# The K-times-probability products of a decode step: one broadcast VectorE instruction of 2048 columns in place of eight of 256

## The chip, the cores and the metric

The kernel runs on one core of one Trainium2 chip. The metric is the device time of one execution in microseconds (us); lower is better. A run's number is the median of its repeated executions.

## The reference

One token passes through attention with a key and value cache, then a gated feed-forward block, and the gradients of everything are wanted as well. The cut that matters:

```
G = 8 groups of 2 query heads, Dh = 256, Sk = 32768 cache rows, only the last W = 4096 rows take part
p  = softmax(q k^T / 16)            # per head, over the 4096 rows
o  = p v ;  out = ... wo ... feed-forward ...
outputs: out_0 (the token), out_1 (its gradient), out_2 and out_3 (gradients of the K and V cache,
         each 8 x 32768 x 256 in bf16, zero outside the last 4096 rows), out_4 .. out_8 (of the weights)
```

So most of the output is zeros: 235 of the 281 MB that the kernel writes are the 28,672 untouched rows of each head group in out_2 and out_3.

## The kernel before

It has three parts. Zero fills of out_2 and out_3 run from the first microseconds to nearly the end; GpSimd issues them. Meanwhile part one goes through the eight groups of heads: scores of a group, softmax, then its "moments" (M = V^T diag(p) K per head, from which later gradients come cheaply). Part two is the projection and the feed-forward. Part three makes the cache gradients of the 4096 rows and the weight gradients and stores them.

The part that the change touches:

```python
        def moments(g, p_f):
            K_sb, V_sb = kv_at(K_off[g]), kv_at(V_off[g])
            M_ps = ps_m.tile([128, 2, 2 * Dh], f32, tag="M")
            for c in range(8):
                pK = pK_slot[c % 2]                    # two buffers of 2048 bf16 columns
                for i in range(4):
                    t = 4 * c + i
                    for hh in range(2):
                        nc.vector.tensor_scalar(out=pK[:, i, hh, :], in0=K_sb[:, t, :], scalar1=p_f[:, 8 * i + c, hh:hh + 1], scalar2=None, op0=ALU.mult)
                for i in range(4):
                    t = 4 * c + i
                    for vh in range(2):
                        nc.tensor.matmul(M_ps[:, vh, :], lhsT=V_sb[:, t, vh * 128:(vh + 1) * 128], rhs=pK[:, i, :, :]..., ...)
            for k, X_sb in enumerate((V_sb, K_sb)):
                for t in range(T):
                    nc.tensor.matmul(ok_ps[:, k, :], lhsT=ppad[g % 2][...], rhs=X_sb[:, t, :], ...)
            # [...] M_ps is copied out
        # [...]
        p_next = scores(0)
        for g in range(G):
            p_f = p_next
            if g + 1 < G:
                p_next = scores(g + 1)
            moments(g, p_f)
            # [...] loads of later K and V; of wo after the last groups
```

The zero fills:

```python
HALF0, HALF1 = 42, 55
    # [...]
    send_fills(0, HALF0)              # each 2 MB, from the whole zeros tile
    send_fills(HALF0, HALF1, True)    # each 2 MB, from the first half of the zeros tile, read twice
    # [...] the second half of the tile meanwhile holds feed-forward weights
            if n == 1:                                          # second block of the feed-forward done
                nc.vector.memset(ar(ZW // 2, ZW // 2), 0.0)     # the second half becomes zeros again
                send_fills(HALF1, len(fills))
```

And the last stage ends with five more zero transfers on SyncE's queue, 18 MB in sum. The order of the instructions on each engine is set by a scheduler when the kernel is built, not by the text above alone.

Of the kernel before, what the change touches and what calls it, by code (L numbers as in the profile page):

```python
# [10 lines left out]
ALU = mybir.AluOpType  # L11
# [6 lines left out]
Dh = 256  # L18
# [15 lines left out]
def kernel(  # L34
        ctx, tc, A_x, A_k_cache, A_v_cache, A_wq, A_wo, B_x, B_w_gate, B_w_up, B_w_down, grad_out,
           out_0, out_1, out_2, out_3, out_4, out_5, out_6, out_7, out_8):
    nc = tc.nc
# [18 lines left out]
    def kv_at(off):  # L56
        return ar(off, T * Dh).rearrange("p (t d) -> p t d", d=Dh)
# [181 lines left out]
    def fill_vpad(i, src):  # L239

        nc.vector.tensor_copy(out=vpad[i][:].rearrange("p e (c w) -> p e c w", w=18)[:, :, :, 0:2],
                              in_=src.unsqueeze(2).to_broadcast([128, 2, 8, 2]))

    def dots(X_sb, XT_slots, pad, rows, cols_pool, cols_tag, evac):

        rows_ps = ps_s.tile([16, 512], f32, tag="rows")
        for q in range(8):
            XT = XT_slots[q % 3]
            tr_ps = ps_tr.tile([128, 2, 4, 128], bf16, tag="tr")
            for dh in range(2):  # L250
                for i in range(4):
                    nc.tensor.transpose(tr_ps[:, dh, i, :], X_sb[:, 4 * q + i, dh * 128:(dh + 1) * 128], ident_bf[:])  # L252
            evac(q, XT, tr_ps[:])
            for dh in range(2):
                nc.tensor.matmul(rows_ps[:], lhsT=pad[:, dh, 16 * q:16 * q + 16], rhs=XT[:, dh].rearrange("p t k -> p (t k)"),  # L255
                                 start=(q == 0 and dh == 0), stop=(q == 7 and dh == 1))
        nc.vector.tensor_copy(out=rows, in_=rows_ps[:])
        cols_ps = cols_pool.tile([128, 4, 8, 2], f32, tag=cols_tag, name="cols_ps")
        for i in range(4):
            nc.tensor.transpose(cols_ps[:, i].rearrange("p c h -> p (c h)"), rows[:, i * 128:(i + 1) * 128], ident_f[0:16, 0:16])  # L260
        return cols_ps
    with tc.tile_pool(name="ps_m", bufs=1, space=bass.MemoryType.PSUM) as ps_m, \
            tc.tile_pool(name="ps_x", bufs=1, space=bass.MemoryType.PSUM) as ps_x, \
            tc.tile_pool(name="ps_c", bufs=1, space=bass.MemoryType.PSUM) as ps_c, \
            tc.tile_pool(name="work1", bufs=2) as work1:

        def scores(g):
            fill_vpad(g % 2, qT_bf[:, 4 * g:4 * g + 4].rearrange("p (k e) -> p e k", e=2))
            sT_ps = dots(kv_at(K_off[g]), KT_slot, vpad[g % 2], rows1, ps_c, "cols", lambda q, XT, ps: nc.scalar.copy(out=XT, in_=ps))  # L269
            pmax = small.tile([16, 1], f32, tag="pmax")  # L270
            nc.vector.reduce_max(out=pmax[:], in_=rows1, axis=AX)
            pmaxT_ps = ps_t.tile([1, 16], f32, tag="tmp")
            nc.tensor.transpose(pmaxT_ps[:], pmax[:], ident_f[0:16, 0:16])
            gmax = small.tile([1, 2], f32, tag="gmax")
            nc.vector.reduce_max(out=gmax[:], in_=pmaxT_ps[:].rearrange("o (c h) -> o h c", h=2), axis=AX)
            nc.vector.tensor_scalar(out=gmax[:], in0=gmax[:], scalar1=-SCALE, scalar2=None, op0=ALU.mult)
            nb_ps = ps_t.tile([128, 2], f32, tag="tmp")
            nc.tensor.matmul(nb_ps[:], lhsT=ones_f[0:1, 0:128], rhs=gmax[:], start=True, stop=True)
            nbias = small.tile([128, 2], f32, tag="nbias")
            nc.vector.tensor_copy(out=nbias[:], in_=nb_ps[:])  # L280
            e_f = work1.tile([128, T, 2], f32, tag="e_f")
            psums = small.tile([128, 2], f32, tag="psums")
            for hh in range(2):
                nc.scalar.activation(out=e_f[:, :, hh], in_=sT_ps[:].rearrange("p i c h -> p (i c) h")[:, :, hh], func=ACT.Exp, bias=nbias[:, hh:hh + 1], scale=SCALE,
                                     accum_out=psums[:, hh:hh + 1])
            tot_ps = ps_t.tile([128, 2], f32, tag="tmp")
            nc.tensor.matmul(tot_ps[:], lhsT=ones_f[:, :], rhs=psums[:], start=True, stop=True)
            rsum = small.tile([128, 2], f32, tag="rsum")
            nc.vector.reciprocal(out=rsum[:], in_=tot_ps[:])
            nc.vector.tensor_tensor(out=pT_all[:, g], in0=e_f[:], in1=rsum[:].unsqueeze(1).to_broadcast([128, T, 2]), op=ALU.mult)  # L290
            p_f = work1.tile([128, T, 2], f32, tag="p_f")
            nc.vector.tensor_copy(out=p_f[:], in_=pT_all[:, g])
            pp = ppad[g % 2]
            if g > 1:
                nc.vector.memset(pp[:, :, 2 * g - 4:2 * g - 2], 0.0)
            nc.vector.tensor_copy(out=pp[:, :, 2 * g:2 * g + 2], in_=pT_all[:, g])  # L296
            return p_f

        def moments(g, p_f):
            K_sb, V_sb = kv_at(K_off[g]), kv_at(V_off[g])  # L300
            M_ps = ps_m.tile([128, 2, 2 * Dh], f32, tag="M")
            for c in range(8):
                pK = pK_slot[c % 2]
                for i in range(4):
                    t = 4 * c + i
                    for hh in range(2):
                        nc.vector.tensor_scalar(out=pK[:, i, hh, :], in0=K_sb[:, t, :], scalar1=p_f[:, 8 * i + c, hh:hh + 1], scalar2=None, op0=ALU.mult)  # L307
                for i in range(4):
                    t = 4 * c + i
                    for vh in range(2):  # L310
                        nc.tensor.matmul(M_ps[:, vh, :], lhsT=V_sb[:, t, vh * 128:(vh + 1) * 128], rhs=pK[:, i, :, :].rearrange("p h d -> p (h d)"),  # L311
                                         start=(t == 0), stop=(t == T - 1))
            for k, X_sb in enumerate((V_sb, K_sb)):
                for t in range(T):
                    nc.tensor.matmul(ok_ps[:, k, :], lhsT=ppad[g % 2][:, 8 * (t % 4) + t // 4, :], rhs=X_sb[:, t, :],  # L315
                                     start=(g == 0 and k == 0 and t == 0), stop=(g == G - 1 and k == 1 and t == T - 1))
            for vh in range(2):
                nc.scalar.copy(out=M_sb[g][:, vh].rearrange("p h d -> p (h d)"), in_=M_ps[:, vh, :])  # L318

        def load_wo(n):  # L320
            LD.dma_start(out=wo_sb[:, 16 * n:16 * n + 16, :], in_=A_wo.rearrange("(p j) n -> p j n", j=32)[:, 16 * n:16 * n + 16, :])

        ok_ps = ps_x.tile([H, 2, Dh], f32, tag="ok")
        after = {0: [("K", 3), ("V", 3)], 1: [("K", 4), ("V", 4), ("K", 5)], 2: [("V", 5)], 3: [("V", 6), ("K", 6)], 4: [("K", 7)], 5: [("V", 7)]}
# [6 lines that stand above are left out]
            for kind, n in after.get(g, []):  # L331
                if kind == "K":
                    load_kv(K_off[n], A_k_cache, n)
                else:
                    load_kv(V_off[n], A_v_cache, n)
            if g == G - 2:
                load_wo(0)
        nc.vector.tensor_copy(out=ok_rows, in_=ok_ps[:])
# [19 lines left out]
    with tc.tile_pool(name="ps_mid", bufs=3, space=bass.MemoryType.PSUM) as ps_mid, \  # L358
# [34 lines left out]
        for n in range(len(BLOCKS)):  # L393
# [3 lines left out]
            for b in range(nb):  # L397
                nc.vector.tensor_tensor_reduce(out=dgb[:, 0:D], in0=wd[:, b, :], in1=dh2_bc[:], scale=1.0, scalar=0.0,
                                               op0=ALU.mult, op1=ALU.add, accum_out=d_hh[:, b0 + b:b0 + b + 1])
# [11 lines left out]
            for i in range(2):  # L411
                nc.vector.tensor_tensor(out=diag[:, 0:w].rearrange("p (m b) -> p m b", b=nb), in0=ident_f[:].unsqueeze(2).to_broadcast([128, 128, nb]),
                                        in1=dgu_f[:, i, cs].unsqueeze(1).to_broadcast([128, 128, nb]), op=ALU.mult)
# [6 lines left out]
            for c in range(4):  # L420
# [3 lines left out]
                                               op0=ALU.mult, op1=ALU.add, accum_out=dhn[0:kp, c, n:n + 1])  # L424
# [28 lines left out]
        for jc in range(32):  # L453
            nc.vector.tensor_tensor_reduce(out=wo_sb[:, jc, :], in0=wo_sb[:, jc, :], in1=dh_bc[:], scale=1.0, scalar=0.0,  # L454
                                           op0=ALU.mult, op1=ALU.add, accum_out=doX_f[:, jc:jc + 1])
# [3 lines left out]
                                in1=m8_f[:].unsqueeze(2).to_broadcast([128, 8, 32]), op=ALU.mult)  # L459
# [13 lines left out]
        for dh in range(2):  # L473
# [11 lines left out]
                                scalar1=SCALE, scalar2=None, op0=ALU.mult)  # L485
# [4 lines left out]
    with tc.tile_pool(name="work2", bufs=2) as work2, tc.tile_pool(name="lnw", bufs=1) as lnw, \  # L490
# [17 lines left out]
        for c in range(3):  # L508
            nc.vector.tensor_tensor_reduce(out=wq2A[:, c, :], in0=wq2A[:, c, :], in1=dq_bc, scale=1.0, scalar=0.0,  # L509
                                           op0=ALU.mult, op1=ALU.add, accum_out=dn1[:, c:c + 1])  # L510
        for h in range(2):
            nc.vector.tensor_tensor_reduce(out=wq2A[:, 0, 0:HJ], in0=wq2B, in1=dq_bc[:, h * HJ:(h + 1) * HJ], scale=1.0, scalar=0.0,
                                           op0=ALU.mult, op1=ALU.add, accum_out=dn1[:, 3 + h:4 + h])
# [86 lines left out]
        for it, g in enumerate(order):  # L600
# [3 lines left out]
            def evac(q, XT, ps):  # L604
                if q % 2:
                    nc.scalar.copy(out=XT, in_=ps)  # L606
                else:
# [7 lines left out]
                                    in1=delta_bc[:, 2 * g:2 * g + 2].unsqueeze(1).to_broadcast([128, T, 2]), op=ALU.subtract)  # L615
# [17 lines left out]
            for l in range(8):  # L633
                for qp in range(2):
# [5 lines left out]
                    t = 4 * l + 2 * qp  # L640
# [47 lines left out]
```

## Time and profile before

802.11 us, median of 3 runs (801.46 to 802.81).

| what | before |
|---|---|
| bytes moved, mean rate | 334.84 MB, 418 GB/s |
| TensorE, VectorE, ScalarE busy | 57%, 46%, 25% of the span |
| last VectorE instruction ends | 719.8 us of 800.5 |
| product stage | 59 to 301 us |

The transfers bound this kernel: no slice but the first and the last is under 409 GB/s. VectorE (DVE) waits 67 us in the product stage for TensorE to free a product buffer.

From the windows table of before, one whole group of heads, then the end of the run (stretch, its length, busy us of PE, PEld, DVE, ACT, POOL with counts, then the clock granted to TensorE, the DMA share, GB/s):

```profile
187.50:219.00 31.50, 31.31 (x224) 16.86 (x222) 15.39 (x75) 9.60 (x15) 3.20 (x6) 1.00 1.00 426
...
750.00:785.00 35.00, 0.00 (x0) 0.00 (x0) 0.00 (x0) 0.00 (x0) 0.00 (x0) 0.50 1.00 430
785.00:790.00 5.00, 0.00 (x0) 0.00 (x0) 0.00 (x0) 0.00 (x0) 0.00 (x0) 0.50 0.74 315
790.00:795.00 5.00, 0.00 (x0) 0.00 (x0) 0.00 (x0) 0.00 (x0) 0.00 (x0) 0.50 0.18 75
795.00:800.50 5.50, 0.00 (x0) 0.00 (x0) 0.00 (x0) 0.00 (x0) 0.00 (x0) 0.50 0.04 18
```

In the product stage TensorE is full and VectorE half full.

From the timeline of before (start us, length us, engine, line, what, count): 26 products in a row, the first five zero fills after GpSimd (POOL) had waited 26.28 us for the refill of the zeros tile, and the last VectorE instruction.

```profile
204.58 5.18 DVE L307 TENSOR_SCALAR arena<-arena,p_f 128x256 bf16<-128x256 bf16 x26
...
374.61 2.65 POOL L132 DMA_DIRECT2D out_dram<-arena  x5 [26.28 <-DVE arena L428]
...
719.12 0.68 DVE L646 CAST arena<-d_ps 128x512 bf16<-128x512 f32 x1
```

### The profile page before, as it was taken

How to read it: one execution, taken by the hardware profiler on the slowest of the kernel's cores; microseconds unless marked ns; L12 is line 12 of the kernel's file. 1: busy time of each engine (PE TensorE's matmuls, PEld its weight loads, DVE VectorE, ACT ScalarE, POOL GpSimd, SP SyncE). 2: the span in 40 equal slices, each digit the busy share in tenths (PEclk: the TensorE clock that was granted, in tenths of full speed). 3: DMA queues.
4: the chain of work that ended last, by engine and by line, in shares of the span. 5: the costliest groups of instructions: out<-in, count | busy, mean ns of one | idle time of the engine just before them, and what ended most of it. 6: DMA issues, size and time to landing. Idle time of an engine off the chain costs nothing.

```text
span 800.5 us, 8486 instructions
## 1 busy us (share of the span) xinstructions
PE 459.3 (57%) x3182; PEld 245.9 (31%) x3182; DVE 370.2 (46%) x1176; ACT 196.3 (25%) x309; POOL 62.0 (8%) x112
## 2 busy tenths in 40 slices
PE   0459999999999994623239295845262064520000
PEld 0334554545545552312129143322021022200000
DVE  2115363472552652255770975766681187660000
ACT  0143313224133100000002054643241045340000
POOL 4000000010100110101100010000000000000000
PEclk9978999999999997555559699776557567655555
DMA  9999999999999999999999999999999999999994
GB/s 350 431 430 429 428 430 430 427 428 428 431 426 422 428 417 409 420 422 428 433 423 425 424 430 428 429 426 426 424 427 423 426 420 425 423 424 427 423 440 192
DMA packets 29359, 334.84 MB, mean 418 GB/s; under 512 B 2819, under 2 KB 5894, under 8 KB 7814
## 3 DMA queue, kind: packets, MB, share of 16 engines
q0 software_dynamic: 16496, 216.01, 63.8%
q1 hardware_dynamic: 11382, 116.68, 34.7%
q10 hardware_dynamic: 1440, 1.61, 0.6%
q8 instruction: 25, 0.41, 0.2%
q14 instruction: 16, 0.13, 0.0%
HBM read 53.69 MB, written 280.59 MB: 418 GB/s over the span
## 4 chain that ended last, share of the span: by engine, by line
PE 35%; DMA 33%; DVE 15%; ACT 4%; issue 2%; another core or an unknown queue 0%; SPq 0%; ACTq 0%; DVEq 0%
DMA out_dram<-arena 19%; PE M_ps L311 11%; PE ok_ps L315 6%; PE rows_ps L255 6%; PE tr_ps L252 4%; DMA dh_bc<-in_grad_out_dram 4%; DMA arena<-in_A_k_cache_dram 4%; ACT arena L269 2%; DMA arena<-in_A_wo_dram 2%; DVE arena L645 2%; DVE arena L454 2%; DVE arena L646 2%; DMA arena<-in_B_w_up_dram 2%; PE dqb_ps L497 2%; DMA arena<-in_B_w_gate_dram 2%; DVE arena L509 2%
## 5 line engine op out<-in xcount | busy, mean ns | idle before, releaser
L307 DVE TENSOR_SCALAR arena<-arena,p_f 128x256 bf16<-128x256 bf16 x512 | 109.8, 280 | 67.0 <-PE M_ps L311 67.0
L311 PE MATMUL M_ps<-arena 128*128 128x512 bf16 x512 | 122.9, 381 | 0.0
L255 PE MATMUL rows_ps<-arena,vpad 128*16 128x512 bf16 x256 | 85.9, 431 | 22.2 <-DVE arena L608 16.9
L252 PE MATMUL tr_ps<-ident_bf,arena 128*128 128x128 bf16 x1024 | 87.9, 236 | 15.0 <-DMA arena<-in_A_k_cache_dram 8.4
L132 POOL DMA_DIRECT2D out_dram<-arena x90 | 48.8, 544 | 560.7 <-DMA out_dram<-arena 522.7
L252 PEld LDWEIGHTS <-arena 128*128 128x128 bf16 x1024 | 65.9, 105 | 65.0 <-issue 55.4
L638 PE MATMUL d_ps<-arena,rT 32*128 32x512 bf16 x256 | 43.6, 511 | 69.6 <-DVE arena L646 50.2
L269 ACT COPY arena<-tr_ps 128x1024 bf16<-128x1024 bf16 x64 | 61.7, 1015 | 87.9 <-PE tr_ps L252 87.9
L311 PEld LDWEIGHTS <-arena 128*128 128x128 bf16 x512 | 46.2, 99 | 50.8 <-issue 6.5
L315 PE MATMUL ok_ps<-arena 128*16 128x256 bf16 x512 | 57.5, 273 | 0.9 <-DVE arena L296 0.9
L606 ACT COPY arena<-tr_ps 128x1024 bf16<-128x1024 bf16 x32 | 32.5, 1016 | 96.1 <-PE tr_ps L252 39.3
L642 ACT CAST arena<-d_ps 128x512 bf16<-128x512 f32 x64 | 37.6, 588 | 71.5 <-PE d_ps L638 71.5
L645 DVE CAST arena<-d_ps 128x512 bf16<-128x512 f32 x64 | 43.9, 686 | 14.9 <-PE d_ps L638 14.6
L315 PEld LDWEIGHTS <-arena 128*16 128x16 bf16 x512 | 45.4, 90 | 13.9 <-issue 3.4
L646 DVE CAST arena<-d_ps 128x512 bf16<-128x512 f32 x64 | 43.5, 680 | 8.3 <-DMA out_dram<-arena 8.3
L638 PEld LDWEIGHTS <-rT 32*128 32x128 bf16 x256 | 11.2, 95 | 95.4 <-issue 52.1
L643 ACT CAST arena<-d_ps 128x512 bf16<-128x512 f32 x64 | 38.0, 594 | 9.1 <-DMA out_dram<-arena 9.1
L255 PEld LDWEIGHTS <-vpad 128*16 128x16 bf16 x256 | 18.9, 91 | 57.1 <-issue 49.3
L318 ACT COPY arena<-M_ps 128x512 f32<-128x512 f32 x16 | 8.6, 589 | 75.0 <-PE M_ps L311 75.0
L509 DVE CUSTOM_DVE_ANT_0 arena<-arena 128x4096 bf16<-128x4096 bf16 x3 | 13.1, 4422 | 23.1 <-ACT arena L502 23.1
L608 DVE COPY arena<-tr_ps 128x1024 bf16<-128x1024 bf16 x32 | 21.7, 680 | 4.1 <-PE tr_ps L252 4.0
L631 DVE TENSOR_SCALAR arena<-R_sb,tl_f 128x512 bf16<-128x512 bf16 x64 | 17.8, 347 | 2.1 <-ACT R_sb L628 1.9
(198 smaller groups left out, 358.1 us busy)
## 6 DMA issues: line engine op xcount, KB each, us to landing
out_dram<-arena POOLq DMA_DIRECT2D x103, 2048.0 KB, 53.5
out_dram<-arena SPq DMA_DIRECT2D x18, 2048.0 KB, 32.7
arena<-in_A_v_cache_dram SPq DMA_DIRECT2D x10, 2048.0 KB, 49.6
arena<-in_A_k_cache_dram SPq DMA_DIRECT2D x8, 2048.0 KB, 29.7
out_dram<-arena SPq DMA_DIRECT2D x4, 4096.0 KB, 57.2
arena<-in_A_wq_dram SPq DMA_DIRECT2D x2, 3072.0 KB, 20.5
arena<-in_A_wo_dram SPq DMA_DIRECT2D x2, 1792.0 KB, 16.2
out_dram<-arena SPq DMA_DIRECT2D x2, 1792.0 KB, 33.2
```

The lines of the kernel that those rows point to most:

```text
L132: ZQ.dma_start(out=reg, in_=zeros)
L252: nc.tensor.transpose(tr_ps[:, dh, i, :], X_sb[:, 4 * q + i, dh * 128:(dh + 1) * 128], ident_bf[:])
L255: nc.tensor.matmul(rows_ps[:], lhsT=pad[:, dh, 16 * q:16 * q + 16], rhs=XT[:, dh].rearrange("p t k -> p (t k)"), start=(q == 0 and dh == 0 ...
L269: sT_ps = dots(kv_at(K_off[g]), KT_slot, vpad[g % 2], rows1, ps_c, "cols", lambda q, XT, ps: nc.scalar.copy(out=XT, in_=ps))
L307: nc.vector.tensor_scalar(out=pK[:, i, hh, :], in0=K_sb[:, t, :], scalar1=p_f[:, 8 * i + c, hh:hh + 1], scalar2=None, op0=ALU.mult)
L311: nc.tensor.matmul(M_ps[:, vh, :], lhsT=V_sb[:, t, vh * 128:(vh + 1) * 128], rhs=pK[:, i, :, :].rearrange("p h d -> p (h d)"), start=(t == ...
L315: nc.tensor.matmul(ok_ps[:, k, :], lhsT=ppad[g % 2][:, 8 * (t % 4) + t // 4, :], rhs=X_sb[:, t, :], start=(g == 0 and k == 0 and t == 0), ...
L638: nc.tensor.matmul(d_ps[:, qi].rearrange("p w d -> p (w d)"), lhsT=rT[32 * q:32 * (q + 1), :], rhs=RB_[32 * q:32 * (q + 1), l, :], start=T ...
L642: nc.scalar.copy(out=stV[:, t:t + 2, :], in_=d_ps[:, :, 0, :])
L643: nc.scalar.copy(out=stK[:, t:t + 2, :], in_=d_ps[:, :, 1, :])
L645: nc.vector.tensor_copy(out=stV[:, t:t + 2, :], in_=d_ps[:, :, 0, :])
L646: nc.vector.tensor_copy(out=stK[:, t:t + 2, :], in_=d_ps[:, :, 1, :])
```

## The change

The intent: eight instructions per chunk, each paying its fixed cost, become one with both operands broadcast by zero strides.

```diff
             for c in range(8):
                 pK = pK_slot[c % 2]
-                for i in range(4):
-                    t = 4 * c + i
-                    for hh in range(2):
-                        nc.vector.tensor_scalar(out=pK[:, i, hh, :], in0=K_sb[:, t, :], scalar1=p_f[:, 8 * i + c, hh:hh + 1], scalar2=None, op0=ALU.mult)
+                nc.vector.tensor_tensor(out=pK, in0=K_sb[:, 4 * c:4 * c + 4, :].unsqueeze(2).to_broadcast([128, 4, 2, Dh]),
+                                        in1=p_f[:, c::8, :].unsqueeze(3).to_broadcast([128, 4, 2, Dh]), op=ALU.mult)
```

## The prediction

> **What bounds the kernel now.** The transfers. The page's 40 slices show the DMA engines at 9 tenths or more in every slice but the last, at 409 to 440 GB/s from the second on. 334.84 MB have to move; at about 427 GB/s that is 784 us, and the first 20 us run at 351 GB/s, the last 20 us at about 200. The zero fills issued by GpSimd (216 MB) stand ready from the start and take up what the compute stages leave unused: GpSimd waits 523 us for earlier fills to land. In the timeline the last VectorE instruction ends at 719.8 us; the last 80 us are transfers alone. The Trainium skill ("Trainium Kernel Development and Optimization", Key Constraints) says that the queues of all engines run on the same 16 DMA engines; the trace agrees, total GB/s stays flat whichever queue is fed.
>
> **The stage changed.** The K products run from 59 to 292 us. There TensorE is the busy engine (windows table: 31.3 of 31.5 us for one group of heads); VectorE is busy 15.4 us of each group, and idles 67 us in total waiting for TensorE to free a product buffer.
>
> **What changes.** 512 instructions of 256 columns (280 ns each; 26 in a row take 5.18 us, so 0.20 us start to start, 1.6 us per chunk of eight) become 64 of 2048. One source is float32, so I expect one column per cycle. The Trainium skill ("VectorE: DVE Perf Modes", the perf-mode tier table) puts fp32 tensor_tensor at 1x, 2293 ns for 2048 columns, bf16 tensor_scalar at 4x. The trace agrees on the slopes: existing tensor_tensors with float32 sources take 687 ns at 512 and 820 ns at 640 columns, 1.04 ns per column; the tensor_scalar goes from 280 to 347 ns for 256 more, 0.26 ns per column. Extrapolated: 2.29 us each, 2.2 us start to start. So VectorE gets slower, despite 448 fewer instructions: from 109.8 to about 146 us in sum, some 4.8 us more per group of heads, 20 of 31 us. Still under TensorE.
>
> The scheduler moves things: the small softmax instructions now stand one by one between products, and TensorE's ok matmuls (0.11 us each), until now a block at each group's end, are spread between chunks of M matmuls (8 x 0.216 us). Putting the trace's durations on the new order by hand, TensorE hardly stalls: a group grows by 0.3 to 1 us, the last (with no scores to interleave) by 1 to 2 us. The product stage ends some 3 to 10 us later than 301 us.
>
> **On the critical path:** almost nothing. Fills move earlier meanwhile, loads and stores later; bytes and rate stay. After compute's end about 18 MB of queued stores (42 us) have to follow, so I estimate that compute could end roughly 25 us later before the DMA engines run out of work. A delay of 3 to 10 us disappears there.
>
> **Predicted: 802.5 us, 80% range 800 to 805.** Faster by over 2%: 0.01; within 2%: 0.96; slower by over 2%: 0.03.
>
> **What would show it right:** the new group at 64 instructions of 2.2 to 2.35 us; VectorE's wait for M matmuls much below 67 us; the attention output projection (ao matmuls) 3 to 10 us later; last VectorE instruction at 723 to 732 us; GB/s per slice unchanged to the last slice.
>
> **What would make it wrong:** zero-stride operands make the instruction cost over 3.5 us, so that VectorE bounds the stage (over 3 us more per group, slack used up); the in-order queue ties softmax and products into long stalls; the order in which the last stores drain shifts the end either way. If it runs at two columns per cycle, VectorE gains, and still nothing shows.

## More of the kernel before

From the profile page of before: the span, the share of time that the DMA engines are busy in 40 slices (9 is 90% or more), the rate per slice, the queues (packets, MB, share of the engines' time), and the groups of the product and of the M matmuls. In a group the columns are line, engine, operation, output<-input, shapes, count, then total busy us, mean ns of one, then the idle time before them and who ended it.

```profile
span 800.5 us, 8486 instructions
DMA  9999999999999999999999999999999999999994
GB/s 350 431 430 429 428 430 430 427 428 428 431 426 422 428 417 409 420 422 428 433 423 425 424 430 428 429 426 426 424 427 423 426 420 425 423 424 427 423 440 192
...
q0 software_dynamic: 16496, 216.01, 63.8%
q1 hardware_dynamic: 11382, 116.68, 34.7%
...
q8 instruction: 25, 0.41, 0.2%
q14 instruction: 16, 0.13, 0.0%
...
L307 DVE TENSOR_SCALAR arena<-arena,p_f 128x256 bf16<-128x256 bf16 x512 | 109.8, 280 | 67.0 <-PE M_ps L311 67.0
L311 PE MATMUL M_ps<-arena 128*128 128x512 bf16 x512 | 122.9, 381 | 0.0
```

## The result, and the profile after

800.03 us, median of 4 runs (799.84 to 800.16); before in the same round 801.81 us (801.46 to 802.81). The ratio is 0.9976, 95% interval 0.9958 to 0.9993. A ratio here is the mean time of one kernel's runs over that of the other's of the same rounds, so it is not quite the ratio of the medians. In two later rounds on other occasions it was 0.9978 and 0.9973. So the change makes the kernel about 2 us, a quarter of a per cent, faster.

From the profile page of after, the same lines:

```profile
span 798.4 us, 7905 instructions
DMA  9999999999999999999999999999999999999996
GB/s 351 429 432 429 430 430 429 429 429 427 429 422 425 426 419 417 413 423 424 422 423 408 430 429 429 432 424 428 423 429 420 426 424 427 419 424 426 427 436 261
...
q0 software_dynamic: 16496, 216.01, 64.0%
q1 hardware_dynamic: 11382, 116.68, 34.8%
...
q8 instruction: 25, 0.41, 0.2%
q14 instruction: 11, 0.09, 0.0%
...
L304 DVE TENSOR_TENSOR arena<-arena,p_f 128x2048 bf16<-128x2048 bf16 x64 | 145.2, 2284 | 58.7 <-PE M_ps L309 58.7
L309 PE MATMUL M_ps<-arena 128*128 128x512 bf16 x489 | 126.4, 381 | 1.1
```

(The page shows 489 of the 512 M matmuls; 23 records are missing from this trace.) VectorE got slower, as predicted: 145.2 us where there were 109.8, 2.28 us each. Its wait for TensorE fell only from 67.0 to 58.7 us. The data queues q0 and q1 carry the same packets. Two counts differ: q14 brought 11 packets of instructions instead of 16, and the program ran 558 instructions fewer (8486 before; 7905 and the 23 missing ones after).

From the windows table of after:

```profile
187.50:219.00 31.50, 31.15 (x209) 15.34 (x210) 19.41 (x20) 9.43 (x14) 3.01 (x6) 1.00 1.01 428
...
750.00:785.00 35.00, 0.00 (x0) 0.00 (x0) 0.00 (x0) 0.00 (x0) 0.00 (x0) 0.50 1.01 434
785.00:790.00 5.00, 0.00 (x0) 0.00 (x0) 0.00 (x0) 0.00 (x0) 0.00 (x0) 0.50 0.85 364
790.00:795.00 5.00, 0.00 (x0) 0.00 (x0) 0.00 (x0) 0.00 (x0) 0.00 (x0) 0.50 0.23 98
795.00:798.40 3.40, 0.00 (x0) 0.00 (x0) 0.00 (x0) 0.00 (x0) 0.00 (x0) 0.50 0.02 10
```

From the timeline of after: three of the new products in the middle of a group, and the last VectorE instruction.

```profile
196.90 2.29 DVE L304 TENSOR_TENSOR arena<-arena,p_f 128x2048 bf16<-128x2048 bf16 x1 [7.10 <-PE M_ps L309]
201.77 0.68 DVE L257 COPY arena<-rows_ps 16x512 f32<-16x512 f32 x1 [2.58 <-PE rows_ps L255]
202.38 2.27 DVE L304 TENSOR_TENSOR arena<-arena,p_f 128x2048 bf16<-128x2048 bf16 x1
...
727.75 0.68 DVE L644 CAST arena<-d_ps 128x512 bf16<-128x512 f32 x1
```

So compute does everything later: the matmuls of the attention output projection start at 311.9 us instead of 304.9, VectorE's last instruction ends at 728.4 instead of 719.8. The kernel still ends 2 us earlier, after 70 us in which nothing but transfers runs. The gain must lie in the transfers, and the bytes of data are the same.

**How uneven the 16 engines end.** A fill of 128 rows is 128 packets of 16 KB and 16 packets of 4 bytes in the packet records, and its landing is recorded as 16 increments of one semaphore: 16 equal shares, one per engine. I took, for each transfer, how far its last share landed behind the median share. The numbers below are worked out from the landing records of the profiled executions:

```
                                        before    after
fills landing in 150 to 200 us, mean      2.4       2.1   us from the median share to the last
fills landing in 250 to 300 us, mean      7.1       5.2
last transfer of the kernel               9.3       5.8
   (its second-last share                 5.6       2.4)
   (its median share lands at           800.6     802.0   us on the trace's own clock, about 10.6 us ahead of the span's)
```

(The two windows are on the trace's own clock, by the median share.) In two other traces of after the last transfer's last share is 5.9 and 6.6 us behind, in experiment 6, which runs like before, 9.4. One engine falls behind the others from the product stage on, and the kernel ends when that one ends. In after it falls behind less. The median engine of after is not earlier; in this trace it is 1.4 us later. Only the last one is earlier.

That gives the theory to be tested.

- **Fetch theory.** Instructions are themselves brought in by the DMA engines (q8, q14). The change takes away 448 instructions and about 110 waits that stood as instructions of their own (the profile counts 152 for the old product line, 43 for the new one). At 64 bytes each (the Trainium skill, "Perfetto Trace Analysis", The 4-stage abstract model) that is, as an estimate, 36 KB, 4.4 packets of 8 KB; q14 has five fewer. In before's records such a packet takes 0.31 us of an engine's time. If they all burden the engine that ends last, the kernel ends 1.5 us or more earlier; spread over 16 engines it would be 0.1 us.
- **Rival.** The product stage ends 7 us later, loads and stores shift against the zero fills, and the engines happen to end more evenly.

### The profile page after: what moved, and what is told of

Read it like the earlier page. It is cut to its first block, busy times and chain, and to the rows that moved or that the text cites. A ratio compares the mean times of both kernels' runs of the same rounds, so it can differ in the third digit from the quotient of the medians. Undisturbed runs are those within 1.5% of the kernel's fastest.

```text
span 798.4 us, 7905 instructions
## 1 busy us (share of the span) xinstructions
PE 469.3 (59%) x3159; PEld 242.1 (30%) x3182; DVE 408.4 (51%) x728; ACT 196.2 (25%) x309; POOL 61.4 (8%) x112
## 4 chain that ended last, share of the span: by engine, by line
PE 40%; DMA 28%; DVE 15%; ACT 4%; issue 2%; another core or an unknown queue 0%; SPq 0%; ACTq 0%; DVEq 0%
DMA out_dram<-arena 18%; PE M_ps L309 13%; PE ok_ps L313 8%; PE rows_ps L255 7%; PE tr_ps L252 5%; DMA dh_bc<-in_grad_out_dram 4%; ACT arena L269 3%; DVE arena L643 2%; DVE arena L644 2%; DMA arena<-in_A_wo_dram 2%; DVE arena L452 2%; PE dqb_ps L495 2%; DMA arena<-in_B_w_up_dram 2%; DMA arena<-in_B_w_gate_dram 2%; DVE arena L421 2%
## 5 line engine op out<-in xcount | busy, mean ns | idle before, releaser
L304 DVE TENSOR_TENSOR arena<-arena,p_f 128x2048 bf16<-128x2048 bf16 x64 | 145.2, 2284 | 58.7 <-PE M_ps L309 58.7
L309 PE MATMUL M_ps<-arena 128*128 128x512 bf16 x489 | 126.4, 381 | 1.1
L252 PEld LDWEIGHTS <-arena 128*128 128x128 bf16 x1024 | 66.0, 105 | 63.5 <-issue 55.6
L313 PE MATMUL ok_ps<-arena 128*16 128x256 bf16 x512 | 64.6, 273 | 1.1 <-DVE arena L296 0.9
L309 PEld LDWEIGHTS <-arena 128*128 128x128 bf16 x512 | 43.3, 99 | 51.0 <-issue 15.3
L313 PEld LDWEIGHTS <-arena 128*16 128x16 bf16 x512 | 41.9, 89 | 29.9 <-issue 21.0
L284 ACT ACTIVATE e_f<-cols_ps,nbias 128x32 f32<-128x32 f32 x16 | 4.5, 286 | 85.7 <-DVE nbias L280 85.7
L257 DVE COPY arena<-rows_ps 16x512 f32<-16x512 f32 x16 | 10.8, 675 | 28.7 <-PE rows_ps L255 28.7
```

Source lines behind the costliest of these rows:

```text
L252: nc.tensor.transpose(tr_ps[:, dh, i, :], X_sb[:, 4 * q + i, dh * 128:(dh + 1) * 128], ident_bf[:])
L304: nc.vector.tensor_tensor(out=pK, in0=K_sb[:, 4 * c:4 * c + 4, :].unsqueeze(2).to_broadcast([128, 4, 2, Dh]), in1=p_f[:, c::8, :].unsqueez ...
L313: nc.tensor.matmul(ok_ps[:, k, :], lhsT=ppad[g % 2][:, 8 * (t % 4) + t // 4, :], rhs=X_sb[:, t, :], start=(g == 0 and k == 0 and t == 0), ...
```

## The experiments

All outputs are right. Experiments 1 to 10 settle what the 2 us depend on. Where they arise stands at the end of this section, and it goes against the fetch theory. Kernels are compared only within the same rounds.

### 1. Give after its instructions back, where they can't touch compute

```diff
+        pad_t = const.tile([128, 8], bf16, name="pad_t")
+        for k in range(560):     # at the very end of the kernel after; reads what the last stage wrote
+            nc.vector.tensor_copy(out=pad_t[:, k % 8:k % 8 + 1], in_=stK[:, T - 1, k % 256:k % 256 + 1])
```

> The kernel after, with 560 VectorE copies of one column each behind its last product of the whole program, while only transfers are left: about as many VectorE instructions and waits as the change took away (448 and about 110), none of them near any compute. Fetch theory (the 1.8 us come from instruction fetches of VectorE, 8 KB packets of 0.31 us, of which the trace of after has five or six fewer, if they lie on the DMA engine that ends last): the time goes back to 801.3 to 802.0 us, ratio to before 0.999 to 1.0005, and four or five more 8 KB fetch packets. Rival (the shifted order of loads and stores levels the 16 engines' ends): the time stays at 800.0 us, ratio 0.9976.

Measured: 802.06 us, ratio to before 0.9997 (0.9985 to 1.001), before 802.19 in these rounds. The gain is gone. The copies ran from 727.3 us on for 34 us, beside transfers alone. In this kernel the product stage is as late as in after and the instruction count is that of before, and the time is that of before: the shift of the loads and stores is worth nothing that these rounds resolve. The queue table of this kernel:

```profile
q8 instruction: 25, 0.41, 0.2%
q14 instruction: 16, 0.13, 0.0%
```

Five packets of 8 KB and 560 instructions, and the 2 us are back. The run does not tell the packets from the instructions.

### 2. The same copies on before

The edit is that of experiment 1, on the kernel before.

> The kernel before, with the same 560 VectorE copies of one column behind its last compute. Fetch theory: 1.3 to 1.7 us slower than before, about 803.3 us, ratio 1.002, with four or five more 8 KB fetch packets. Rival: as before, 801.8 us, ratio 1.000.

Measured: 804.63 us, ratio 1.0029 (1.0016 to 1.0041). The direction and the packets are as the fetch theory had them: its queue table has 20 packets on q14 where before has 16. The size, 2.4 us, is over the 1.3 to 1.7 us expected: 0.6 us per packet, twice the 0.31 us that a packet's record takes, or 4.4 ns per instruction.

### 3. The same number of instructions on GpSimd

The copies of experiment 1 with `nc.gpsimd` in place of `nc.vector`.

> The kernel after, with 560 one-column copies behind its last compute on GpSimd in place of VectorE. Fetch theory: whether the time goes up depends on which DMA engine fetches for GpSimd; if on the one that ends last, 801.5 us, else 800.0 us. Rival: 800.0 us.

Measured: 801.97 us, ratio 0.9996 (0.9983 to 1.001), q14 at 15 packets. It is not VectorE's work but the number of instructions: those of another engine, which come over the same queue q14, cost the same.

### 4. Control: VectorE as busy for as long, with 16 instructions

```diff
+        pad_t = const.tile([128, 16], f32, name="pad_t")
+        for k in range(16):      # at the very end of the kernel after
+            nc.vector.reduce_sum(out=pad_t[:, k:k + 1], in_=stK[:, 24:32, :].rearrange('p t d -> p (t d)'), axis=AX)
```

> Control for the 560 copies: the kernel after, with 16 VectorE sums over 2048 columns (about 2.1 us each, 34 us in sum, as long as the 560 copies took) behind its last compute. Same engine busy for the same time in the same stretch, but 16 instructions in place of 560. Fetch theory: at most one fetch packet more, time as after (ratio 0.997 to 0.9985). Rival (a busy VectorE slows the last stores): 2 us over after, ratio 1.000.

Measured: 800.45 us, ratio 0.9977 (0.9963 to 0.999). The 16 sums took 35.2 us from 726.6 us on. A busy VectorE does not slow the last transfers; 560 instructions in the same stretch do.

### 5. After, unchanged

> The kernel after, unchanged, timed again so that it stands on the same chip beside the others of this call. Both theories: ratio to before 0.9965 to 0.9985, about 2 us under before.

Measured: 800.13 us (799.74 to 802.5), ratio 0.9978 (0.9965 to 0.999). One execution, the profiled one, took 802.5 us with the same fetches; in its trace the median share of the last transfer lands 1.6 us later than in after, not the last share alone. I have no cause for it. It is the only such one of the 14 executions of after.

> The kernel after, unchanged, to stand on the same chip beside the others of this call: ratio to before 0.9965 to 0.9985.

Measured: 800.09 us (799.95 to 800.29), ratio 0.9973 (0.9961 to 0.9986).

### 6. The delay alone, a miss

```diff
+        for _ in range(12):
+            nc.vector.memset(ok_rows, 0.0)
         nc.vector.tensor_copy(out=ok_rows, in_=ok_ps[:])     # kernel before, end of the product stage
```

> The kernel before, with 12 VectorE fills of 16 rows by 512 columns (about 0.6 us each) ahead of the copy that ends the product stage, so that everything behind it comes some 7 us later, as in after, with 12 instructions more. Fetch theory: no gain, 801.5 to 802.5 us, ratio 1.000. Rival (later compute reorders loads and stores): about 800 us, ratio 0.9976.

Measured: 802.14 us, ratio 0.9998 (0.9985 to 1.0011). This tells nothing of the delay: VectorE was idle there, ran the fills while it waited, and started the copy at 301.7 us; the last VectorE instruction ended at 719.9 us, as in before. A run of no effect, which shows no more than that 12 instructions don't matter.

### 7. The delay alone, overdone

```diff
                 pK = pK_slot[c % 2]
+                if g == G - 1 and c > 1:
+                    for _ in range(2):
+                        nc.vector.memset(pK, 0.0)
                 for i in range(4):                            # kernel before
```

> The kernel before, with two fills of a product buffer (about 0.9 us each) ahead of each of the last six chunks of the last group: 12 instructions more, and what follows the product stage should come 6 to 10 us later, as in after; delay_before had not managed that, its fills ran while VectorE was idle. Fetch theory: no gain from the delay, ratio to before 0.999 to 1.001. Rival (later loads and stores level the engines' ends): ratio 0.9976.

Measured: 807.13 us, ratio 1.0067 (1.0055 to 1.008). Neither theory had that. The delay came out at 17 us, not 6 to 10 (last VectorE instruction at 736.5 us), and the transfers have a hole. From the windows table of this kernel:

```profile
370.00:380.00 10.00, 1.32 (x9) 0.68 (x8) 0.07 (x1) 0.65 (x2) 0.00 (x0) 0.50 1.03 422
380.00:385.00 5.00, 2.95 (x36) 2.62 (x34) 1.64 (x4) 0.00 (x0) 0.00 (x0) 0.50 0.54 228
385.00:390.00 5.00, 0.00 (x0) 0.00 (x0) 4.59 (x8) 0.00 (x0) 0.00 (x0) 0.50 0.04 18
390.00:395.00 5.00, 2.28 (x8) 0.82 (x9) 4.90 (x17) 1.01 (x1) 4.20 (x8) 0.50 0.66 262
```

The share of the DMA engines (the last column but one) falls to 0.04. GpSimd had sent all fills that need only half of the zeros tile by 345 us and then waited 45 us for VectorE to refill the other half; then, at 390.7 us, it sent eight at once, with the DMA engines empty. After itself was not far from this. From its timeline, the first fills behind the refill:

```profile
381.23 3.68 POOL L132 DMA_DIRECT2D out_dram<-arena  x7 [36.89 <-DVE arena L426]
```

Seven at once, so if eight is the most it keeps under way, one was left; in before it was five, at 374.6 us. In the hole the missing share adds up to 2.3 + 4.8 + 1.7 = 8.8 us of a fully used stretch, more than the 4.8 us that the kernel lost; the 16 engines ended more evenly here (last share 3.1 us behind the median), which may be the rest.

### 8. The same delay with more half fills

```diff
-HALF0, HALF1 = 42, 55
+HALF0, HALF1 = 42, 60          # on the kernel of experiment 7
```

> The kernel of delay_products_before (807.1 us, with a hole of about 9 us in the transfers near 385 us) with 18 instead of 13 of the zero fills that read only the first half of the zeros tile, which the second half's refill need not precede. If the hole was GpSimd running out of fills it could send while it waited for that refill: no slice under 400 GB/s in 300 to 700 us, 801.5 to 803.5 us, ratio to before 0.999 to 1.0015. If the delay costs by itself: 806 to 807 us again.

Measured: 801.61 us, ratio 0.9999 (0.9986 to 1.0013). The hole is gone, from its windows table:

```profile
380.00:385.00 5.00, 2.33 (x28) 2.05 (x27) 2.27 (x4) 0.00 (x0) 0.00 (x0) 0.50 1.00 424
385.00:390.00 5.00, 0.00 (x0) 0.00 (x0) 4.58 (x9) 0.00 (x0) 0.00 (x0) 0.50 1.01 428
```

Two things follow. First, the hole was the zeros tile and nothing else. Second, this is the delay alone that experiments 6 and 7 had missed, at about twice the size it has in after: compute ends almost 17 us later than in before (last VectorE instruction at 736.4 us), with the instructions of before and 12 more, q14 at 16 packets, and the time is that of before. A delay brings no gain here, which leaves the rival theory without support.

### 9. Another queue of instructions: TensorE's

```diff
+        pad_ps = ps_t.tile([1, 8], f32, tag="tmp", name="pad_ps")
+        for k in range(512):     # at the very end of the kernel after
+            nc.tensor.matmul(pad_ps[:, k % 8:k % 8 + 1], lhsT=stK[:, T - 1, k % 256:k % 256 + 1], rhs=stK[:, T - 1, 0:1], start=True, stop=True)
```

> The kernel after, with 512 matmuls of one column behind its last compute: 1024 TensorE instructions, 64 KB, four fetches of 16 KB of TensorE's own queue (0.93 us each in the traces). If TensorE's fetches burden the engine that ends last as VectorE's do: 3 to 4.5 us over after, ratio to before 1.001 to 1.003. If they are spread over the engines or lie on another: as after, ratio 0.9976, at most 0.5 us more.

Measured: 803.00 us, ratio 1.0006 (0.9994 to 1.0019), 2.9 us over after in the same rounds, with 29 packets of 16 KB on q8 where after has 25. That is 0.7 us for each of the four, under the 0.93 us that one takes in the records, and just under the range; per instruction it is 2.8 ns. TensorE's instructions cost the end as well. Its timeline shows also that they were probably not there in time: TensorE stopped for 3 to 5 us, first after 224 of these matmuls and then after each 128 (256 instructions, 16 KB), and a 16 KB packet of q8 falls in each of the three stops, at 731.5, 739.9 and 747.2 us.

```profile
725.06 5.74 PE L660 MATMUL pad_ps<-arena 128*1 128x1 bf16 x224 [1.21 <-ACT arena L641]
733.98 3.34 PE L660 MATMUL pad_ps<-arena 128*1 128x1 bf16 x128 [3.18 <-issue]
742.09 3.34 PE L660 MATMUL pad_ps<-arena 128*1 128x1 bf16 x128 [4.78 <-issue]
749.38 0.94 PE L660 MATMUL pad_ps<-arena 128*1 128x1 bf16 x32 [3.95 <-issue]
```

### 10. A half step of the change: four products of 512 columns

```diff
-                nc.vector.tensor_tensor(out=pK, in0=K_sb[:, 4 * c:4 * c + 4, :]..., in1=p_f[:, c::8, :]..., op=ALU.mult)
+                for i in range(4):
+                    nc.vector.tensor_tensor(out=pK[:, i], in0=K_sb[:, 4 * c + i, :].unsqueeze(1).to_broadcast([128, 2, Dh]),
+                                            in1=p_f[:, 8 * i + c, :].unsqueeze(2).to_broadcast([128, 2, Dh]), op=ALU.mult)
```

> The kernel after with four products of 512 columns per chunk instead of one of 2048: 256 instructions where after has 64 and before 512[...]. Fetch theory: 192 instructions of 64 bytes are 1.5 fetches of 8 KB; at 0.4 to 0.5 us each 0.5 to 1 us over after, between after and before (ratio 0.998 to 0.9995). Rival (something in the wide instruction itself or in the delay of the stage): as after, ratio 0.9976.

Measured: 801.06 us, ratio 0.9988 (0.9975 to 1.0), with 14 packets on q14: between after (11 packets, 800.09 us in the same rounds) and before (16 packets, 802.13 us). The expectation had counted the 192 products alone; the waits that stand as instructions of their own are 152 here and 43 in after, so 301 instructions came on top, 3.2 ns each. VectorE needs still more time for these than for the wide ones (161.5 us, 687 ns each), and the time follows the instructions, not VectorE. The interval reaches both neighbours' values nearly, so this run supports that and would not carry it alone.

### 11. Further the same way

Three more groups of per-row products in the last stage become broadcast products, on the kernel after:

```diff
-                for j in range(16):
-                    scale_into(buf[:, j * D:(j + 1) * D], dh_bc[:], oX_f[:, 16 * n + j:16 * n + j + 1])
+                for j in range(0, 16, 4):
+                    scale_rows(buf[:, j * D:(j + 4) * D], dh_bc[:], oX_f[:, 16 * n + j:16 * n + j + 4])
 # [...] likewise 14 products of 448 columns as 2, and 64 of 512 columns as 16;
 # scale_rows is one tensor_tensor with both operands broadcast
```

> The kernel after with three more groups of per-row products made of broadcast products: 32 of 448 columns become 8, 14 become 2, 64 of 512 become 16, so 84 VectorE instructions less, some of them slower. Fetch theory: 84 instructions are 0.65 of a fetch: 0 to 0.5 us under after, 799.5 to 800.2 us, ratio 0.997 to 0.9976, hard to tell from after; it should at least not be slower. Rival: as after.

Measured: 799.75 us (799.51 to 800.09), ratio 0.9969 (0.9957 to 0.9982). It is the fastest kernel, but 0.3 us under after is not resolved by the intervals, and q14 has 11 packets, as in after: 84 instructions are less than one packet. So this small gain, if it is one, does not come from fetch packets; 84 instructions at the 2.8 to 4.4 ns of the other runs would be 0.2 to 0.4 us (an estimate).

All runs but experiment 7, whose hole hides the rest, in one table (before and after of the same rounds where there are any). The instructions are those that the profile counts, waits included (7905 of after's 7928 in its first trace):

| kernel | instructions | q14 packets | us | ratio to before |
|---|---|---|---|---|
| before | 8486 | 16 | 801.8 to 802.3 (medians of four rounds) | 1 |
| after | 7928 | 11 | 800.03, 800.13, 800.09 | 0.9976, 0.9978, 0.9973 |
| after, fewer products later | 7839 | 11 | 799.75 | 0.9969 |
| after, 16 wide sums at the end | 7945 | 11 | 800.45 | 0.9977 |
| after, products of 512 | 8230 | 14 | 801.06 | 0.9988 |
| after, 560 GpSimd copies at the end | 8489 | 15 | 801.97 | 0.9996 |
| after, 560 VectorE copies at the end | 8488 | 16 | 802.06 | 0.9997 |
| after, 512 matmuls at the end | 8952 | 11 (and 4 more on q8) | 803.00 | 1.0006 |
| before, 12 idle fills | 8490 | 16 | 802.14 | 0.9998 |
| before, 17 us later, more half fills | 8477 | 16 | 801.61 | 0.9999 |
| before, 560 VectorE copies at the end | 9046 | 20 | 804.63 | 1.0029 |

The time follows the number of instructions, and the packets follow it too, so this table cannot tell the two apart.

**Where the fetch packets lie.** The packet records don't name their engine, but their times give it away. Near the end each packet starts 3 or 4 ns (in places 1 to 16) before another one ends, so the packets can be strung into 16 chains, one an engine. The last transfers have eight packets of one size and one of 4 bytes on each engine, in the same order, which leaves one way back from the last packet to about 745 us (two in after, 5 ns apart in the last column). "Longer" is against the usual 611 ns of a 16 KB packet and 1213 ns of a 32 KB packet. Worked out from the packet records:

```
the engine that ends last           fetch packets in the    of these      its data packets
(followed back to, us)              stretch, all engines    on it         longer by, in sum
before (745.6)                             0                   0            0.00 us
after (743.5)                              0                   0            0.02
after, 16 wide sums (743.5)                0                   0            0.02
after, 560 VectorE copies (744.3)          3                   0            1.04
after, 560 GpSimd copies (743.9)           3                   0            1.49
before, 560 VectorE copies (747.8)         1                   0            0.40
after, 512 matmuls (746.6)                 2                   0            0.16
```

So the fetch packets are not what delays the end: they lie on other engines. On the engine that ends last the data packets themselves take longer, and only while instructions run: with the VectorE copies, which end at 761.3 us, each packet up to there is longer (a 16 KB one by some 20 to 50 ns), and none behind. About 280 copies fall in the stretch, 3.7 ns each; for 560 that makes 2.1 us (an estimate), what the copies cost. The product stage looks the same, though chains strung over so long a stretch are a best fit and not the only one: between 60 and 300 us the engine that lags has none of the fetch packets of q8 and q14, in before as in after, and its data packets are longer by 8.1 us in sum in before and by 6.6 us in after.

What an instruction does to that engine is not shown. A rival that no run tests is the profiler itself: every timed execution lists a span and a granted clock, so none is known to have run unrecorded. If the records of the instructions load that engine, the 2 us would not be there without the profiler.

## Why the prediction was right or wrong

- **What bounds the kernel, and where the change acts: right.** The transfers bound it; compute came 8.6 us later at its end and that cost nothing.
- **The cost of the new instruction: right.** 2.2 to 2.35 us were predicted; it is 2.28 us, 145.2 us in sum against "about 146". The Trainium skill ("VectorE: DVE Perf Modes", the perf-mode tier table) has 2293 ns for this shape with fp32; the trace agrees within 1%, zero strides and mixed types included. The merge made this work of VectorE a third longer.
- **The delay of the product stage: right in size.** Predicted 3 to 10 us, measured 7.0 us at the start of the projection; VectorE's last instruction was predicted at 723 to 732 us and ended at 728.4.
- **VectorE's wait for TensorE "much below 67 us": wrong.** It is 58.7 us. It idles where TensorE works on the next group's scores: the timeline of after has 7.10 us idle in one piece before one product, and in that stretch TensorE does transposes and score matmuls, with only the eight M matmuls of one chunk between them.
- **"Bytes and rate stay", so "almost nothing" on the critical path: the step that failed.** I counted 448 instructions less as VectorE's fixed cost, found that it was outweighed by the lost mode, and stopped. But each instruction that runs, on VectorE, GpSimd or TensorE, also costs the end of the transfers 2.8 to 4.4 ns in these runs, and the change takes away 558 (448 products and 109 waits, and one more). Giving them back at a harmless place gives the 2 us back (experiment 1), on either of two engines (3), while neither a busy VectorE (4) nor a delay (8) does. I had predicted 802.5 us, slightly slower than before, and the kernel became 1.8 to 2.2 us faster; that 800.03 us still lies at the edge of 800 to 805 is luck. The sign of the small effect was wrong, because its one term that reaches the end was missing from the sum. My first account of this term, the five fetch packets, failed as well: they lie on other engines than the one that ends last.
- **"GB/s per slice unchanged to the last slice": wrong in the last slice**, 261 against 192 GB/s. I took the end of the transfers as total bytes over total rate. The kernel ends with its last engine, 9.3 us behind the median share in before and 5.8 us in after. What burdens that engine counts in full.
- **The slack of "roughly 25 us": right at the end, wrong on the way.** A 17 us later end of compute cost nothing at the end (8), but the same delay emptied the queues near 385 us until more half fills were given (7). I had looked for the slack only where the kernel ends, not at the wait of GpSimd that the waits view lists with 26.3 us.

What stays open: that the number of instructions makes the 2 us is shown, and that they arise as longer data packets on the DMA engine that ends last, not as fetch packets. Why an instruction makes them longer, and whether it does so without the profiler, is not.

## What to carry to other kernels

When the transfers bound a kernel, an off-path engine's instructions may not be free: here each cost 2.8 to 4.4 ns at the end, and whether it would without the profiler is untested. Look at the last few microseconds of the DMA share, where one engine of 16 can hold the end. And before a count that fits the time, such as the fetch packets here, is called the cause, look whether it lies on the engine that ends last. A merge of instructions can be worth it though the engine itself gets slower. And look for slack at every point where a long-running stream of transfers waits for compute, not only at the end.

## What the Trainium skill lacked or had wrong

- "Runtime: NRT & Kernel Launch", Instruction fetch mechanics, says that instructions are fetched in 16 KiB blocks over the sequencer's own DMA queue. Here q8 (TensorE) shows 16 KB packets, but q14, which grew with VectorE's and with GpSimd's instructions alike, shows 8 KB packets.
- The same section calls fetching hidden by the speed of dispatch. With one-column matmuls beside a full DMA load TensorE stood still for 3 to 5 us, first after 448 instructions and then after each 256, with a 16 KB packet of q8 in each stop.
- No page that I found says that the number of instructions can show in the end of the transfers: 558 fewer are 2 us of 802 here. "DMA: Bandwidth & Descriptors" would be the place. It has a row for refill among the queue rows of the 16 engines and calls two engines usually slower, but gives neither a cost per instruction nor one per fetch; here the last share of the last transfer landed 9.3 us behind the median share, 5.8 us with 558 instructions fewer.
